# Moving three weight requests in the load order of a chunk-selecting attention and soft-MoE kernel

## The chip, the cores and the metric

The kernel runs on one core of one Trainium2 chip. The metric is device time in microseconds (us), lower is better; a run's figure is the median over its executions. The profiled execution is one more execution of the same program, with its own time and its own span (first to last instruction of the program).

## The reference

Inputs are `q`, `k`, `v` of shape 4 x 8 x 768 x 64 (batch, heads, positions, head size) and the MoE's `phi` (512 x 32), `w1` (8 x 512 x 1024) and `w2` (8 x 1024 x 512), all float32.

```python
# attention: every query keeps the 6 best of 24 chunks of 32 keys
k_min, k_max = min and max of k over each chunk
ub = sum_d max(q * k_min, q * k_max);  ub = where(causal chunk, ub, -1e9)
top_chunks = argsort(ub)[..., -6:]
scores = where(chosen chunk and causal, q @ k.T / 8, -1e9)
attn = softmax(scores) @ v
x = attn as 3072 rows of 512
# soft MoE with 32 slots, 4 to an expert
logits = x @ phi
d = softmax of logits over the rows;   slot_input = d.T @ x
slot_out[e] = relu(slot_input[e] @ w1[e]) @ w2[e]     for the 8 experts
c = softmax of logits over the slots;  out = c @ slot_out
```

## The kernel before

Two heads of one batch form a **pair**; there are 16 pairs, numbered 0 to 15 in the code and here. Written k10 or v3, a load is that of pair 10's `k` or pair 3's `v`; w0 to w15 are the 16 expert weights in the order in which they are asked for (w0 to w7 are `w1`, w8 to w15 are `w2`).

All loads are DMAs that GpSimd (POOL) issues, in the order in which they stand in its instruction stream, and they cast float32 to bf16 on the way. `load(i, "k")` and `load(i, "q")` (L141) fetch 192 KB as written, `load_v(i)` (L149) as much in smaller pieces, `load_w(i)` (L131) 1024 KB. `k_in` and `q_in` have three buffers each, `v_t` four; each of the first 14 weights has its own place, w14 and w15 take the place of pools that are closed near the end. Each issue on POOL also waits until the issue eight before it has landed, since the DMAs take turns on eight semaphores.

The order of work is written out by hand (a manual schedule), engine by engine. A prologue prepares pairs 0 and 1 and makes the masks; then a loop runs i from 1 to 15. Iteration i computes the scores of pair i in six groups (`scores`, L303 and L313; `expo`, the exponential on ScalarE, L327; `mask`, POOL, L337), applies the weights of pair i-1 to `v` (`pv`, L355), chooses the chunks of pair i+1 (`ubound` L255 and L262, `select` L274 to L277, `ns_transposes` L285), transposes and evacuates k and q of pair i+2 (`transposes` L211, `evac_T` L220, `kmin` L229, `kmax` L235), normalises pair i-2 (L368) and asks for k and q of pair i+4 and v of pair i+2. The MoE's steps for a batch run in the iterations after its last pair.

`weights(i)` (L537) asks for as many weights as `wplan` says for iteration i, after `load_v(i + 2)`; the entry 0 is served in iteration 1:

```python
wplan = {0: 1, 2: 1, 3: 1, 4: 1, 5: 1, 7: 1, 8: 1, 9: 1, 10: 1, 11: 1, 12: 1, 13: 2, 14: 1, 15: 1}
```

With w0, asked for in the prologue, that makes 16. After the loop the experts run: `experts_in` (L800) with w0 to w7, `experts_out` (L838) with w8 to w14, `last_expert_out` (L849) with w15. Then the 3072 output rows are formed and written by DMAs from the SyncE queue.

Of the kernel before, what the change touches and what calls it, by code (L numbers as in the profile page):

```python
# [60 lines left out]
def kernel(  # L61
# [69 lines left out]
    def load_w(i):  # L131

        if i < E:
            src = moe_w1[i].rearrange("(a p x) f -> p a (x f)", p=P, x=2)
            dst = w_sb[i].rearrange("p (a f) -> p a f", a=NDG // 2)
        else:
            src = moe_w2[i - E].rearrange("(a p x) d -> p a (x d)", p=P, x=4)
            dst = w_sb[i].rearrange("p (a f) -> p a f", a=NFG // 4)
        nc.gpsimd.dma_start(out=dst, in_=src)  # L139

    def load(i, nm):  # L141

        b, j = divmod(i, NPB)
        t = inp.tile([P, 2, NQT * D], BF16, name=nm + "_in", tag=nm + "_in")
        src = {"k": k, "q": q}[nm][b, 2 * j:2 * j + 2]
        nc.gpsimd.dma_start(out=t, in_=src.rearrange("h (p g) d -> p h (g d)", p=P))  # L146
        st[nm, i] = t

    def load_v(i):  # L149
        b, j = divmod(i, NPB)  # L150
        nc.gpsimd.dma_start(  # L151
            out=v_t[i % NV][:, :, :, :D],
            in_=v[b, 2 * j:2 * j + 2].rearrange("h (g p) d -> p h g d", p=P),
        )
# [14 lines left out]
    for j in range(4):  # L169
# [8 lines left out]
        pattern=[[-CH, 2], [-64, 2], [0, NCHUNK]], channel_multiplier=1,  # L178
    )
    load(1, "q")  # L180
    nc.gpsimd.affine_select(
        out=qgrp, in_=qgrp, compare_op=ALU.not_equal, fill=1.0, base=0,
        pattern=[[-1, 4], [0, CH]], channel_multiplier=1,
# [8 lines left out]
    def spread_mask(t0, t1):  # L192
        nc.scalar.copy(
            smask[:, :, t0:t1].rearrange("p o t a x -> p o (t a) x"),
            schunk[:, :, 4 * t0:4 * t1].broadcast_to([P, 2, 4 * (t1 - t0), CH]),
        )
# [3 lines left out]
    def warm(n):  # L200
        r = ones_sq.rearrange("p (o c) -> p o c", o=1).broadcast_to([P, 4, P])
        for _ in range(n):
            nc.tensor.matmul(warm_ps, lhsT=ones_sq, rhs=r, start=True, stop=True)

    def transposes(i, nm):

        ps = p_tp.tile([P, NQT, P], BF16, name="tr_ps", tag="tp")
        src = st.pop((nm, i))
        for g in range(NQT):
            for h in range(2):  # L210
                nc.tensor.matmul(  # L211
                    ps[h * 64:(h + 1) * 64, g, :], lhsT=src[:, h, g * D:(g + 1) * D], rhs=ident,
                    is_transpose=True,
                )
        st[nm + "ps", i] = ps
# [53 lines left out]
    def select(i):  # L269
        ub = st.pop(("ubps", i)).rearrange("p j h x c -> p (j h x) c")  # L270
        mx = tpu.tile([P, NQT * 2, 8], F32, name="mx", tag="mx")
        for a in range(NQT * 2):
            t = a // 4 + NJ * (a % 2)
            nc.vector.max(mx[:, a, :], ub[:, a, :max(8, 4 * t + 4)])  # L274
        ns = ns_t[i % 2].rearrange("p j h x c -> p (j h x) c")
        nc.gpsimd.tensor_copy(ns[:, :, NCHUNK:NCHUNK + 1], mx[:, :, 0:1])
        nc.vector.tensor_tensor(  # L277
            ns[:, :, :NCHUNK], ub,
            mx[:, :, TOPK - 1:TOPK].broadcast_to([P, NQT * 2, NCHUNK]), op=ALU.is_lt,
        )  # L280
# [250 lines left out]
            step(i // NPB)  # L531


    wplan = {0: 1, 2: 1, 3: 1, 4: 1, 5: 1, 7: 1, 8: 1, 9: 1, 10: 1, 11: 1, 12: 1, 13: 2, 14: 1, 15: 1}
    nw = 1

    def weights(i):  # L537
# [19 lines left out]
    ubound(0)  # L557
    load(3, "k")
    load(3, "q")
    load_v(0)  # L560
    transposes(1, "q")
    evac_T(1, "q")
    spread_mask(NJ, NQT)
    select(0)
    load_v(1)
    warm(5)
    ns_transposes(0)
# [3 lines left out]
    qsplit(1)  # L571
    nc.gpsimd.dma_start(out=phi_sb, in_=moe_phi.rearrange("(hg p) s -> p hg s", p=P))
    make_identity(nc, identf)
    load_w(0)
    load(4, "k")
    load(4, "q")

# [368 lines left out]
```

## Time and profile before

| what | value |
|---|---|
| median of 3 runs | 162.14 us (161.63 to 162.91) |
| profiled execution, its own time | 162.55 us |
| its span | 160.8 us |
| mean granted TensorE clock | 0.979 |
| busy PE, DVE, ACT, POOL | 138.5, 121.4, 122.8, 102.7 us |
| read from HBM, written | 52.49 MB, 6.29 MB |
| DMA queue of the POOL loads | 38416 packets, 26.25 MB as written to the core's memory |

The profile's engines are PE (TensorE matmul), PEld (its weight loads), DVE (VectorE), ACT (ScalarE), POOL (GpSimd) and SP (SyncE). In the timeline a row has start, duration, engine, line, operation, tiles, shape and count, and in brackets how long the engine stood idle before it and what ended that. The DMA issues have the time from the start of the issue to the landing. The table of stretches has each engine's busy time, the granted clock, the busy share of the 16 DMA engines and the GB/s that they wrote.

### The profile page before, as it was taken

What the parts mean: (1) busy time and instruction counts of PE and PEld (TensorE: products, weight loads), DVE (VectorE), ACT (ScalarE), POOL (GpSimd) and SP (SyncE); (2) the same over time, 40 slices, a digit from 0 to 9 for tenths busy, and PEclk for the clock granted to TensorE, in tenths of its full rate; (3) what the DMA queues carried; (4) which work ended last, traced back from release to release, by engine and by line L of the source; (5) the groups of instructions that cost most, each with busy time, mean ns of one, the idle gap of its engine ahead of it and who ended that gap; (6) DMA issues with size and microseconds to landing.
All of it is one profiled execution on the core that took longest, in us unless ns stands there. A gap on an engine that the chain in (4) does not pass through costs nothing.

```text
span 160.8 us, 5896 instructions
## 1 busy us (share of the span) xinstructions
PE 138.5 (86%) x2420; PEld 91.7 (57%) x2420; DVE 121.4 (75%) x433; ACT 122.8 (76%) x169; POOL 102.7 (64%) x203
## 2 busy tenths in 40 slices
PE   7786799999999998999999899969899999987500
PEld 2343366766767686666768576646676854542100
DVE  4465989999999989998988899968862660187620
ACT  3679899999999898999989889968788521166520
POOL 7999577989888696988968986829864800000000
PEclk9999999999999999999999999999999999999965
DMA  3999999999999999999999999999999999329996
GB/s 40 141 120 158 206 197 206 201 182 211 194 210 196 209 200 206 198 182 211 197 210 195 214 191 212 195 207 197 209 203 214 213 217 213 67 71 415 419 419 248
DMA packets 40603, 32.92 MB, mean 205 GB/s; under 512 B 26368, under 2 KB 34816, under 8 KB 40576
## 3 DMA queue, kind: packets, MB, share of 16 engines
q0 software_dynamic: 38416, 26.25, 110.3%
q1 hardware_dynamic: 2160, 6.29, 9.7%
q8 instruction: 19, 0.31, 0.7%
q14 instruction: 8, 0.07, 0.1%
HBM read 52.49 MB, written 6.29 MB: 366 GB/s over the span
## 4 chain that ended last, share of the span: by engine, by line
PE 39%; DMA 23%; ACT 14%; DVE 11%; issue 5%; POOL 4%; DVEq 0%; ACTq 0%; POOLq 0%
DMA k_in<-in_k_dram 15%; ACT e_sb L327 8%; PE sc_ps L303 6%; PE at_ps L355 6%; DMA out_dram<-o_sb 5%; PE sc_ps L313 5%; PE tr_ps L211 4%; PE xT_ps L377 3%; DMA q_in<-in_q_dram 3%; ACT qT L220 3%; DVE mx L274 3%; PE h_ps L800 2%; PE so_ps L838 2%; DVE x_sb L368 2%; PE ub_ps L262 1%
## 5 line engine op out<-in xcount | busy, mean ns | idle before, releaser
L327 ACT ACTIVATE e_sb<-sc_ps 128x1024 bf16<-128x1024 f32 (+1 forms) x96 | 83.1, 917 | 7.1 <-PE sc_ps L313 6.5
L337 POOL TENSOR_SCALAR_AFFINE_SELECT e_sb<-e_sb 128x256 bf16<-128x256 bf16 x96 | 38.1, 414 | 18.5 <-ACT e_sb L327 18.0
L303 PE MATMUL sc_ps<-qT,kT 64*128 64x384 bf16 (+3 forms) x258 | 36.8, 305 | 2.5 <-ACT e_sb L327 1.6
L313 PE MATMUL sc_ps<-nsT,smask 64*128 64x384 bf16 (+2 forms) x294 | 38.1, 284 | 0.1
L355 PE MATMUL at_ps<-v_t,e_sb 128*128 128x65 bf16 x672 | 29.7, 194 | 1.9 <-DVE x_sb L368 1.5
L355 PEld LDWEIGHTS <-e_sb 128*128 128x128 bf16 x672 | 25.6, 98 | 4.1 <-issue 2.6
L274 DVE MAX8 mx<-ub_ps 128x8 f32<-128x8 f32 (+1 forms) x192 | 16.8, 162 | 4.2 <-PE ub_ps L262 4.2
L303 PEld LDWEIGHTS <-kT 64*128 64x128 bf16 x258 | 13.9, 93 | 10.7 <-issue 5.3
L313 PEld LDWEIGHTS <-smask 64*128 64x128 bf16 x294 | 14.9, 94 | 3.9 <-issue 0.6
L151 POOL DMA_DIRECT2D v_t<-in_v_dram x16 | 16.6, 1039 | 0.7 <-PE ns_ps L285 0.5
L229 DVE TENSOR_REDUCE mm<-kT 128x24 bf16<-128x768 bf16 x16 | 15.1, 945 | 2.3 <-ACT kT L220 2.3
L220 ACT COPY kT<-tr_ps 128x768 bf16<-128x768 bf16 x16 | 12.8, 802 | 4.8 <-PE tr_ps L211 4.8
L368 DVE TENSOR_TENSOR x_sb<-at_ps,inv 128x768 bf16<-128x768 f32 (+1 forms) x17 | 15.5, 910 | 0.6
L235 DVE TENSOR_REDUCE mm<-kT 128x24 bf16<-128x768 bf16 x16 | 15.1, 942 | 0.0
L220 ACT COPY qT<-tr_ps 128x768 bf16<-128x768 bf16 x16 | 12.8, 799 | 1.7 <-PE tr_ps L211 1.6
L146 POOL DMA_DIRECT2D k_in<-in_k_dram x16 | 11.7, 733 | 0.9 <-POOLq L930 0.8
L139 POOL DMA_DIRECT2D w_sb<-in_moe_w_dram x16 | 11.4, 711 | 0.9 <-DMA w_sb<-in_moe_w_dram 0.7
L146 POOL DMA_DIRECT2D q_in<-in_q_dram x16 | 11.5, 718 | 0.0
L211 PE MATMUL tr_ps<-ident,k_in 128*64 128x128 bf16 x192 | 8.4, 223 | 2.2 <-DMA k_in<-in_k_dram 1.7
L388 DVE COPY xT_sb<-xT_ps 128x768 bf16<-128x768 bf16 (+1 forms) x15 | 8.0, 536 | 2.6 <-PE xT_ps L377 2.6
L211 PE MATMUL tr_ps<-ident,q_in 128*64 128x128 bf16 x192 | 8.4, 223 | 0.8 <-DMA q_in<-in_q_dram 0.6
L377 PE MATMUL xT_ps<-ident,x_sb 128*128 128x128 bf16 x96 | 8.2, 221 | 0.0
(138 smaller groups left out, 202.7 us busy)
## 6 DMA issues: line engine op xcount, KB each, us to landing
w_sb<-in_moe_w_dram POOLq DMA_DIRECT2D x16, 1024.0 KB, 14.8
out_dram<-o_sb SPq DMA_DIRECT2D x10, 512.0 KB, 4.5
k_in<-in_k_dram POOLq DMA_DIRECT2D x16, 192.0 KB, 10.0
q_in<-in_q_dram POOLq DMA_DIRECT2D x16, 192.0 KB, 10.5
v_t<-in_v_dram POOLq DMA_DIRECT2D x16, 192.0 KB, 10.9
out_dram<-o_sb SPq DMA_DIRECT2D x2, 256.0 KB, 4.3
out_dram<-first SPq DMA_DIRECT2D x2, 128.0 KB, 2.0
out_dram<-first SPq DMA_DIRECT2D x1, 256.0 KB, 2.1
```

Source lines behind the costliest of these rows:

```text
L146: nc.gpsimd.dma_start(out=t, in_=src.rearrange("h (p g) d -> p h (g d)", p=P))
L151: nc.gpsimd.dma_start(out=v_t[i % NV][:, :, :, :D], in_=v[b, 2 * j:2 * j + 2].rearrange("h (g p) d -> p h g d", p=P),)
L211: nc.tensor.matmul(ps[h * 64:(h + 1) * 64, g, :], lhsT=src[:, h, g * D:(g + 1) * D], rhs=ident, is_transpose=True,)
L220: nc.scalar.copy(t.rearrange("d (p g) -> d p g", g=NQT), st.pop((nm + "ps", i)).rearrange("d g p -> d p g"),)
L229: nc.vector.tensor_reduce(mm[:, 0, 0, :], kT, axis=AX.X, op=ALU.min)
L274: nc.vector.max(mx[:, a, :], ub[:, a, :max(8, 4 * t + 4)])
L303: nc.tensor.matmul(ps[:, h, c:c + w], lhsT=kT[r, kg * P:(kg + 1) * P], rhs=qT[r, qs], start=True, stop=False,)
L313: nc.tensor.matmul(ps[:, h, c + (f - t0) * P:c + (l - t0) * P], lhsT=smask[r, x, kg].rearrange("p a b -> p (a b)"), rhs=nsT[r, (f - x * NJ ...
L327: nc.scalar.activation(e[:, :, :w], st.pop(("scps", i, g))[:, :, :w], func=ACT.Exp, scale=scale)
L337: nc.gpsimd.affine_select(out=e[:, :, c:c + P], in_=e[:, :, c:c + P], compare_op=ALU.is_ge, fill=0.0, base=0, pattern=[[0, 2], [1, P]], ch ...
L355: nc.tensor.matmul(o, lhsT=st["e", i, g][:, h, c:c + P], rhs=v_t[i % NV][:, h, kg, :], start=(kg == 0), stop=(kg == t),)
L368: nc.vector.tensor_tensor(st["x", b][:, t0:t1, 2 * j:2 * j + 2, :].rearrange("p t h d -> p h t d"), at[:, :, :, :D], inv.broadcast_to([P, ...
```

## The change

w0 is asked for right behind q1 in the prologue, and no longer behind the identity matrix `identf`. `load_v(0)` goes behind `select(0)`, so that POOL's copy in `select(0)` (L276) comes ahead of v0's request. In `wplan` the weight of iteration 5 goes to iteration 6 and that of iteration 10 to iteration 11, which now has two: w5 is asked for behind k10, q10 and v8 (it was ahead of them), w9 behind k15, q15 and v13. The instructions of all engines are the same in number and kind; only POOL's order differs.

```diff
     load(1, "q")
+    load_w(0)
     nc.gpsimd.affine_select(
         out=qgrp, in_=qgrp, ...
@@
-    wplan = {0: 1, 2: 1, 3: 1, 4: 1, 5: 1, 7: 1, 8: 1, 9: 1, 10: 1, 11: 1, 12: 1, 13: 2, 14: 1, 15: 1}
+    wplan = {0: 1, 2: 1, 3: 1, 4: 1, 6: 1, 7: 1, 8: 1, 9: 1, 11: 2, 12: 1, 13: 2, 14: 1, 15: 1}
@@
     load(3, "k")
     load(3, "q")
-    load_v(0)
     transposes(1, "q")
     evac_T(1, "q")
     spread_mask(NJ, NQT)
     select(0)
+    load_v(0)
     load_v(1)
@@
     make_identity(nc, identf)
-    load_w(0)
     load(4, "k")
     load(4, "q")
```

## The prediction

> **What bounds the kernel now.** I read the page's slices first, then the table of stretches, the waits, the timeline around the waits that DMA ends, and the landings.
>
> ```profile
> DMA  3999999999999999999999999999999999329996
> GB/s 40 141 120 158 206 197 206 201 182 211 194 210 196 209 200 206 198 182 211 197 210 195 214 191 212 195 207 197 209 203 214 213 217 213 67 71 415 419 419 248
> ```
>
> ```profile
> core 0: us, PE busy (x) PEld busy (x) DVE busy (x) ACT busy (x) POOL busy (x), PEclk, DMA share, GB/s
> 3.00:6.50 3.50, 2.46 (x21) 0.83 (x20) 0.49 (x3) 1.10 (x2) 3.33 (x9) 1.00 1.15 159
> 6.50:14.00 7.50, 6.15 (x79) 3.29 (x80) 6.25 (x23) 6.10 (x8) 7.26 (x12) 1.00 1.03 126
> 14.00:25.30 11.30, 9.64 (x172) 6.26 (x171) 8.92 (x39) 10.43 (x14) 8.63 (x19) 1.00 1.61 192
> 25.30:60.00 34.70, 34.12 (x669) 24.50 (x667) 33.19 (x118) 33.66 (x46) 29.35 (x57) 1.00 1.35 202
> ```
>
> A slice is 4.0 us. From 16 us to about 136 us the loads flow at some 200 GB/s without a break: in that stretch the stream of loads is one long queue, and its end depends on how soon it fills. Only the start has room: 126 GB/s from 6.5 to 14 us. PE, ACT and DVE are nearly full as well (34.12, 33.66 and 33.19 of 34.70 us), so the kernel has two chains of like length, loads and compute. They meet at two places in the loop and at the end:
>
> ```profile
> PE tr_ps L211 <- DMA k_in<-in_k_dram: 1.7, 2, 1.3
> POOL w_sb L139 <- DMA w_sb<-in_moe_w_dram: 0.7, 1, 0.7
> ```
>
> ```profile
> 57.90 0.74 POOL L146 DMA_DIRECT2D k_in<-in_k_dram  x1
> 69.18 0.53 PE L211 MATMUL tr_ps<-ident,k_in 128*64 128x128 bf16 x12 [0.37 <-DMA k_in<-in_k_dram]
> 69.75 0.80 ACT L220 COPY kT<-tr_ps 128x768 bf16<-128x768 bf16 x1 [0.20 <-PE tr_ps L211]
> 93.29 0.72 POOL L146 DMA_DIRECT2D k_in<-in_k_dram  x1
> 105.99 0.53 PE L211 MATMUL tr_ps<-ident,k_in 128*64 128x128 bf16 x12 [1.30 <-DMA k_in<-in_k_dram]
> 106.56 0.80 ACT L220 COPY kT<-tr_ps 128x768 bf16<-128x768 bf16 x1 [1.13 <-PE tr_ps L211]
> ```
>
> The requests at 57.90 and 93.29 are k10 and k15. PE stands idle 0.37 and 1.30 us for them.
>
> ```profile
> 118.63 0.77 POOL L139 DMA_DIRECT2D w_sb<-in_moe_w_dram  x1
> w_sb<-in_moe_w_dram POOLq DMA_DIRECT2D x1, 1024.0 KB, 21.5
> 138.07 2.34 PE L838 MATMUL so_ps<-w_sb,hT_pad 128*32 128x512 bf16 x34
> 140.21 0.28 PE L849 MATMUL so_last<-w_sb,hT_pad 128*32 128x256 bf16 x1
> 141.42 0.40 PE L849 MATMUL so_ps<-w_sb,hT_pad 128*32 128x256 bf16 x8 [0.37 <-DVE so_part L881]
> ```
>
> w15 is asked for at 118.63 and lands 21.5 us later, at 140.1; its first user L849 starts at 140.21 behind a PE that was busy with L838. So at the end loads and compute arrive within 0.1 us of each other. This is the main reading: shortening compute alone gains nothing, since w15 lands no sooner, and shortening the loads alone gains nothing, since PE arrives no sooner. The change touches both.
>
> **Part 1, w5 and w9 behind k10 and k15.**
>
> ```profile
> 52.23 0.70 POOL L139 DMA_DIRECT2D w_sb<-in_moe_w_dram  x1 [0.70 <-DMA w_sb<-in_moe_w_dram]
> v_t<-in_v_dram POOLq DMA_DIRECT2D x1, 192.0 KB, 13.0
> w_sb<-in_moe_w_dram POOLq DMA_DIRECT2D x1, 1024.0 KB, 15.9
> k_in<-in_k_dram POOLq DMA_DIRECT2D x1, 192.0 KB, 11.2
> 50.50 1.03 POOL L151 DMA_DIRECT2D v_t<-in_v_dram  x1
> 90.00 0.71 POOL L139 DMA_DIRECT2D w_sb<-in_moe_w_dram  x1
> k_in<-in_k_dram POOLq DMA_DIRECT2D x16, 192.0 KB, 10.0
> ```
>
> The three landings of single requests are v7's (50.50 + 13.0 = 63.5), w5's (52.23 + 15.9 = 68.1) and k10's (57.90 + 11.2 = 69.1): they land in the order of their requests, and a weight takes 4.6 us of the queue. Take it from ahead of k10 and k10 lands at about 64.5, some 4 us before PE asks for it. The same holds for k15, which now stands behind w9 (asked for at 90.00). Both waits go: 0.37 + 1.30 = 1.67 us on PE. ACT, next in line, idled 0.20 and 1.13 us, so if ACT and not PE sets the pace behind the waits the gain is 1.33. I take PE's, since its stream is the fuller one in the table (34.12 of 34.70 us): 1.7. The lower bound is ACT's 1.3; the upper one, 2.4, adds POOL's 0.70 below, if the masks that it held up count after all.
>
> What comes later for it: w5 and w9 themselves, by three loads (about 1 + 1 + 1.5 us by the spacing of the queue) which nobody uses before the experts at 132 us. The loads behind them (k11, v14 and so on) stand behind the same bytes as before. POOL's issue of w5 no longer waits 0.70 us for w3; it held up two masks, for which PE shows no wait, so I book nothing. Without part 2, w15 still lands at 140.1, and the gain would end there: within 0.3 us of nothing.
>
> **Part 2, w0 behind q1.**
>
> ```profile
> 4.75 0.74 POOL L146 DMA_DIRECT2D q_in<-in_q_dram  x1
> q_in<-in_q_dram POOLq DMA_DIRECT2D x1, 192.0 KB, 4.3
> 6.29 0.75 POOL L146 DMA_DIRECT2D k_in<-in_k_dram  x1
> k_in<-in_k_dram POOLq DMA_DIRECT2D x1, 192.0 KB, 5.1
> 12.81 0.72 POOL L139 DMA_DIRECT2D w_sb<-in_moe_w_dram  x1
> 14.23 0.72 POOL L146 DMA_DIRECT2D q_in<-in_q_dram  x1
> q_in<-in_q_dram POOLq DMA_DIRECT2D x1, 192.0 KB, 11.1
> ```
>
> q1 lands at 9.05, k2 at 11.4, q4 at 25.3. What stands between q1 and q4 in the queue is the same set in both kernels: w0, three k, three q, v0, v1 and the small phi. With w0 in front, its 1.05 MB are in the queue from about 6.2 us, and the set needs 4.6 + 6 x 1.0 + 2 x 1.5 + 0.2 = 13.8 us at the rates of the loop, so q4 lands at 22.9: the stream comes **2.4 us sooner**. The other way of counting: 7.5 us at 126 instead of 202 GB/s leave 0.57 MB undone, 2.8 us. Lower bound: nothing gained, if the slow stretch is slow whatever is queued. I take 2.4. Later it is kept: a k lands 10.0 us (median of all 16) after its request, so 2.4 us less still leaves the queue filled. Then w15 lands at 137.7, and PE, 1.7 us sooner, wants it at 138.5: both chains are shorter by at least 1.7.
>
> What it costs at the start:
>
> ```profile
> 9.43 0.53 PE L211 MATMUL tr_ps<-ident,q_in 128*64 128x128 bf16 x12 [0.24 <-ACT kT L220]
> 10.35 0.23 POOL L276 CAST ns_t<-mx 128x12 bf16<-128x12 f32 x1 [0.16 <-DVE mx L274]
> 15.95 0.53 PE L211 MATMUL tr_ps<-ident,k_in 128*64 128x128 bf16 x12
> 14.96 1.49 POOL L337 TENSOR_SCALAR_AFFINE_SELECT e_sb<-e_sb 128x256 bf16<-128x256 bf16 x4
> 17.18 0.23 POOL L276 CAST ns_t<-mx 128x12 bf16<-128x12 f32 x1 [0.73 <-DVE mx L274]
> ```
>
> The issue itself takes POOL 0.72 us. It pushes two masks and the four requests k2 to q3, which end at 9.9 instead of 9.2; v0's issue (1.03 us) now follows the copy at 10.35, which still waits for DVE alone. Cost nothing; had v0 stayed, the copy would be 0.7 late. k2 now lands behind w0: 9.05 + 4.6 + 1.0 = 14.6, wanted at 15.95, 1.3 us to spare. POOL also gets two new waits through the turn of eight: k4's issue for w0's landing (13.7, POOL arrives at about 13.8) and q4's for k2's (14.6, arrives 14.6). Queued behind them are the four masks (1.49 us) and the copy at 17.18, which has 0.73 us of idle time before it. So the cover is about 1 us: if w0 lands at 14.7 or later, chunk choice of pair 1 slips, and PE with it. q1 stands ahead of w0 and has 0.35 us. Taken at nothing; the price if cover fails is the third rival's.
>
> **Sum.** 162.55 - 1.7 = 160.85 for the profiled execution (span 159.1). That execution lies 0.41 above the median of the runs, so the median becomes 160.4.
>
> **Rivals.** *First, the start stays slow* (162.0). When k2 and q2 were in transit, four requests stood in the queue (k2 to q3 were issued by 9.17), and yet 6.5 to 14 us ran at 126 GB/s: that speaks for a limit other than the queue's depth. Then w0 moves 0.62 MB by 14 us, the rest at 202 GB/s, and lands at 16.1; k2 follows at 17.1, 1.1 us late; the set as a whole lands no sooner, w15 stays at 140.1 and eats the 1.7. Against it: the share of 1.03 in that stretch says that each DMA engine had one packet in hand, against 1.35 to 1.61 later, which is what thin queues look like, and w0's large pieces are what fills them.
>
> The Trainium skill has a mechanism for this rival (SBUF — State Buffer, "SBUF: two separate sides"): while VectorE runs certain fast modes, GpSimd cannot write the descriptors of its DMAs, and the DMA engines starve. By that rule the start would be slow for any load, and the sum would be the 162.0 of this rival. The trace bears it out little: DVE is busy 6.25 of 7.50 us in the slow stretch but 33.19 of 34.70 us in one that runs at 202 GB/s.
>
> *Second, slower* (164.3). The slow rate lasts until w0 and k2 have landed: w0 at 9.05 + 1.05 MB / 126 GB/s = 17.4, k2 at 19.0. PE stands 3.0 us at 15.95; POOL issues q4 at 19.0, its masks end at 21.2, and the copy of 17.18 comes 4.0 us late, of which some 0.2 are cover. The start slips 3.9, the loop wins back 1.7: +2.2. It decides from a k2 landing of about 16.7 on (slip over 1.7), and is over 1% from 18.5 on. For it: k2 and q2 landed 2 us apart before, where later ones land 1 us apart. Against: the rate had recovered by 14 us by itself.
>
> **How the numbers follow.** The bound of 1%, 1.62 us, is about what a measurement of this kernel can tell from no change. Forecast 0.60, three quarters of it beyond 1.62 us; the first rival 0.22; the second 0.18. Faster 0.45, same 0.15 + 0.22 = 0.37, slower 0.18. The forecast's own range is 159.7 to 161.1 (gains of 2.4 and 1.3 us, with 0.3 more at the upper end for the spread of a median). The whole range starts just below, at 159.6, holds the first rival and goes to 162.8, into the nearer part of the second.
>
> **What would show it.** Right: no idle time of PE before the transposes of k10 and k15; k2's transposes near 16 us as now; the stretch of 6.5 to 14 us near 200 GB/s; w15's landing near 137.7 and L849 near 138.5. Wrong: an idle PE ahead of k2's transposes, the copy L276 of pair 1 later than 17.4, the stretch still near 126 GB/s, or PE idle before L849 until w15 has landed.

## The result and the profile after

| | median | runs |
|---|---|---|
| before | 161.88 us (161.37 to 162.91) | 4 |
| after | 164.12 us (163.98 to 165.37) | 4 |
| ratio | 1.0141, 95% interval 1.0092 to 1.0189 | |
| profiled execution after | 164.01 us, span 162.3 us, mean clock 0.973 | |

The change makes the kernel 1.4% slower. In a second set (E9 below) twelve runs of it had a median of 164.10 us against 162.36 for the kernel before; the ratio of that set, 1.0066 (1.0032 to 1.01), leaves out runs more than 1.5% above the fastest, so it is the lower of the two. Forecast were 160.4 us, with 162.8 as the upper end; what came is close to the second rival (164.3 us).

From L181 to the prologue's later part a line has a number higher by one in the kernel after (L276 is L277, L285 is L286, L211 is L212); the experts' lines keep theirs. The slices of the page after, 4.06 us each:

```profile
GB/s 39 145 194 190 170 158 86 202 187 190 204 198 208 200 206 184 198 202 203 201 203 204 200 204 185 205 213 202 210 195 217 214 214 215 110 62 406 418 420 250
```

The start is fuller than before (194 and 190 where 120 and 158 stood), but there is a hole where before had none: 86 GB/s in the seventh slice, 24.3 to 28.4 us. The table of stretches, with the columns of before:

```profile
6.50:14.00 7.50, 6.36 (x80) 3.27 (x80) 6.20 (x22) 6.12 (x9) 6.62 (x12) 1.00 1.04 175
14.00:25.30 11.30, 7.80 (x117) 4.75 (x114) 6.43 (x34) 7.88 (x10) 6.56 (x14) 0.85 1.57 158
20.00:21.00 1.00, 0.86 (x13) 0.69 (x15) 0.41 (x2) 0.00 (x0) 1.00 (x4) 0.63 2.14 172
21.00:22.00 1.00, 1.00 (x14) 0.48 (x10) 0.97 (x2) 0.62 (x1) 0.77 (x1) 0.50 1.52 189
24.00:25.00 1.00, 1.00 (x28) 0.79 (x26) 0.97 (x12) 0.87 (x2) 0.65 (x2) 1.00 0.53 37
25.00:26.00 1.00, 1.00 (x20) 0.56 (x18) 0.97 (x3) 0.89 (x2) 0.94 (x3) 1.00 0.18 24
```

The stretch of 6.5 to 14 us runs at 175 GB/s instead of 126, and the next one loses it: 158 instead of 192, with PE busy 7.80 us instead of 9.64 and a mean clock of 0.85. The waits of after name the place:

```profile
PE ns_ps L286 <- POOL ns_t L277: 2.0, 1, 2.0
PE tr_ps L212 <- DMA k_in<-in_k_dram: 1.1, 2, 0.9
```

The largest wait of PE is now one for POOL's small copy in `select(1)`. What made the copy late stands in the landings of single requests (w0's, k2's and w15's) and in the timeline:

```profile
w_sb<-in_moe_w_dram POOLq DMA_DIRECT2D x1, 1024.0 KB, 10.7
k_in<-in_k_dram POOLq DMA_DIRECT2D x1, 192.0 KB, 10.2
w_sb<-in_moe_w_dram POOLq DMA_DIRECT2D x1, 1024.0 KB, 21.8
```

```profile
5.48 0.72 POOL L139 DMA_DIRECT2D w_sb<-in_moe_w_dram  x1
6.99 0.74 POOL L146 DMA_DIRECT2D k_in<-in_k_dram  x1
...
16.72 0.72 POOL L146 DMA_DIRECT2D k_in<-in_k_dram  x1 [2.31 <-PE ub_ps L263]
17.18 0.53 PE L212 MATMUL tr_ps<-ident,k_in 128*64 128x128 bf16 x12 [0.89 <-DMA k_in<-in_k_dram]
17.67 0.71 POOL L146 DMA_DIRECT2D q_in<-in_q_dram  x1 [0.24 <-issue]
18.40 1.49 POOL L338 TENSOR_SCALAR_AFFINE_SELECT e_sb<-e_sb 128x256 bf16<-128x256 bf16 x4
19.85 0.23 POOL L277 CAST ns_t<-mx 128x12 bf16<-128x12 f32 x1
20.14 0.41 PE L286 MATMUL ns_ps<-ident,ns_t 128*128 128x128 bf16 x3 [2.00 <-POOL ns_t L277]
23.85 0.53 PE L212 MATMUL tr_ps<-ident,k_in 128*64 128x128 bf16 x12
24.71 0.71 POOL L139 DMA_DIRECT2D w_sb<-in_moe_w_dram  x1
71.54 0.53 PE L212 MATMUL tr_ps<-ident,k_in 128*64 128x128 bf16 x12
107.53 0.53 PE L212 MATMUL tr_ps<-ident,k_in 128*64 128x128 bf16 x12
120.16 0.77 POOL L139 DMA_DIRECT2D w_sb<-in_moe_w_dram  x1
...
142.02 0.56 PE L849 MATMUL so_last<-w_sb,hT_pad 128*32 128x256 bf16 x8
```

w0 lands at 5.48 + 10.7 = 16.2. POOL stands idle 2.31 us ahead of k4's request and starts it at 16.72, 0.5 us after that landing. The row names PE's L263 as what ended the wait; that is an instance of a wait for several things put down to the wrong one, and E5 below names w0. k2 lands at 17.2, 0.9 us after PE asked for it, and q4's request follows 0.5 us behind that. Only then come the masks (18.40) and the copy (19.85 instead of 17.18), and PE begins its L286 at 20.14. Three rows of before to compare with:

```profile
17.75 0.33 PE L285 MATMUL ns_ps<-ident,ns_t 128*128 128x128 bf16 x3 [0.85 <-DVE ns_t L277]
20.85 0.53 PE L211 MATMUL tr_ps<-ident,k_in 128*64 128x128 bf16 x12
21.64 0.72 POOL L139 DMA_DIRECT2D w_sb<-in_moe_w_dram  x1
```

PE is 2.39 us late at its L286, and 3.00 us late at k3's transposes (23.85 against 20.85): it ran through 20 to 24 us at a clock of 0.50 to 0.66, and E9 below shows what that costs. At k10's transposes it is 2.36 late and at k15's 1.54, and the waits that stood there (0.37 and 1.30 us) are gone; L849 starts 1.81 late and the span is 1.5 longer. POOL's next weight request, w1's, is 3.07 us later than before, and by then the queue has run dry: the 37 and 24 GB/s above.

### The profile page after: what moved, and what is told of

The parts are those of the page before. It is cut to its first block, busy times and chain, and to the rows that moved or that the text cites. A ratio compares the mean times of both kernels' runs of the same rounds, so it can differ in the third digit from the quotient of the medians.

```text
span 162.3 us, 5896 instructions
## 1 busy us (share of the span) xinstructions
PE 140.8 (87%) x2420; PEld 92.6 (57%) x2420; DVE 122.5 (75%) x433; ACT 122.7 (76%) x169; POOL 103.0 (63%) x203
## 4 chain that ended last, share of the span: by engine, by line
PE 44%; ACT 18%; DVE 17%; DMA 7%; issue 6%; POOL 4%; DVEq 0%; ACTq 0%; SPq 0%; POOLq 0%
ACT e_sb L328 11%; PE sc_ps L304 8%; PE at_ps L356 6%; PE sc_ps L314 6%; DMA out_dram<-o_sb 5%; PE tr_ps L212 5%; PE xT_ps L378 3%; ACT qT L221 3%; DVE mx L275 3%; PE h_ps L800 2%; PE so_ps L838 2%; DMA k_in<-in_k_dram 2%; DVE x_sb L369 2%; POOL e_sb L338 2%; PE ub_ps L263 2%
## 5 line engine op out<-in xcount | busy, mean ns | idle before, releaser
L304 PE MATMUL sc_ps<-qT,kT 64*128 64x384 bf16 (+3 forms) x258 | 37.3, 309 | 2.5 <-ACT e_sb L328 1.6
L314 PE MATMUL sc_ps<-nsT,smask 64*128 64x384 bf16 (+2 forms) x294 | 38.7, 288 | 0.1
L304 PEld LDWEIGHTS <-kT 64*128 64x128 bf16 x258 | 14.0, 94 | 10.7 <-issue 5.4
L212 PE MATMUL tr_ps<-ident,k_in 128*64 128x128 bf16 x192 | 8.7, 229 | 1.1 <-DMA k_in<-in_k_dram 1.1
L250 DVE TENSOR_SCALAR qpn<-qT 128x768 bf16<-128x768 bf16 x15 | 9.5, 633 | 0.0
L212 PE MATMUL tr_ps<-ident,q_in 128*64 128x128 bf16 x192 | 8.7, 229 | 0.1
```

The source lines that it names most:

```text
L212: nc.tensor.matmul(ps[h * 64:(h + 1) * 64, g, :], lhsT=src[:, h, g * D:(g + 1) * D], rhs=ident, is_transpose=True,)
L304: nc.tensor.matmul(ps[:, h, c:c + w], lhsT=kT[r, kg * P:(kg + 1) * P], rhs=qT[r, qs], start=True, stop=False,)
L314: nc.tensor.matmul(ps[:, h, c + (f - t0) * P:c + (l - t0) * P], lhsT=smask[r, x, kg].rearrange("p a b -> p (a b)"), rhs=nsT[r, (f - x * NJ ...
```

## The experiments

Unless said otherwise the time is the median, and the ratio is to the kernel before, run on the same chip.

**E1, the new `wplan` alone.** Does part 1 do what it says, and what is it worth by itself?

```diff
-    wplan = {..., 5: 1, 7: 1, 8: 1, 9: 1, 10: 1, 11: 1, ...}
+    wplan = {..., 6: 1, 7: 1, 8: 1, 9: 1, 11: 2, ...}
```

> Only the new wplan (w5 behind k10, w9 behind k15); w0 and v0 stay where they were. Theory A (the loss sits at the start, in what w0's place does): not slower than before; PE's idle time of 0.37 and 1.30 us ahead of the transposes of k10 and k15 is gone, and since w15 still lands near 140.1 the gain ends there: 161.3 to 161.9 against 161.9. Rival B (the moved weights of the loop cost the time): slower by 1 us or more, 163 and up. Rival C (w15's landing does not bound the end): the whole 1.7 us are won, 160.2.

Measured: 161.98 us, ratio 0.9967 (0.9941 to 0.9994). The profiled execution:

```profile
104.60 0.53 PE L211 MATMUL tr_ps<-ident,k_in 128*64 128x128 bf16 x12
140.52 0.40 PE L849 MATMUL so_last<-w_sb,hT_pad 128*32 128x256 bf16 x8 [1.07 <-DMA w_sb<-in_moe_w_dram]
140.74 0.40 PE L849 MATMUL so_ps<-w_sb,hT_pad 128*32 128x256 bf16 x8
```

k15's transposes start at 104.60 with no idle time, where before had 105.99 and 1.30. This execution had been 0.28 us later at k2 (16.23 against 15.95), so the two waits gave 1.39 + 0.28 = 1.67 us. At the end PE waits 1.07 us for w15, and most of the gain is lost again; a part stays, since the second half of L849 starts 0.68 us sooner than before (140.74 against 141.42, which had waited for DVE's `so_part`), and the span is 0.4 us shorter. Part 1 alone is 0.33% faster than before (0.37 us by the medians). Of all versions tried it is the only one whose interval lies below 1, but only just, and with so many versions compared one such interval can be chance.

**E2, the start alone** (w0 behind q1, v0 behind `select(0)`, the old `wplan`).

```diff
     load(1, "q")
+    load_w(0)
...
-    load_v(0)
...
     select(0)
+    load_v(0)
...
-    load_w(0)
     load(4, "k")
```

> Only the start of the change (w0 behind q1, v0's request behind select(0)); the old wplan. Theory A: slower by more than the whole change, as the 3 us that pair 1 slips are not won back at k10 and k15, or by as much where those two waits swallow the slip: 164.0 to 165.0. Rival B (the wplan costs): 161.9 or faster.

Measured: 165.24 us, ratio 1.0165 (1.0122 to 1.0208).

```profile
17.82 0.67 PE L212 MATMUL tr_ps<-ident,k_in 128*64 128x128 bf16 x12 [1.62 <-DMA k_in<-in_k_dram]
20.77 0.50 PE L286 MATMUL ns_ps<-ident,ns_t 128*128 128x128 bf16 x3 [1.53 <-POOL ns_t L277]
```

The time is a little above the expected 164.0 to 165.0. The whole loss sits in part 2; k2 comes 1.62 us late and the selection 3.0 us later than before (20.77 against 17.75).

**E3, the change with k4 and q4 asked for behind `select(1)`.** This takes away the two requests that hold up POOL and leaves w0 where the change puts it.

```diff
     make_identity(nc, identf)
-    load(4, "k")
-    load(4, "q")
...
     select(1)
+    load(4, "k")
+    load(4, "q")
```

> The whole change, but k4 and q4 are asked for behind POOL's copy of select(1) instead of ahead of the masks of pair 0, so that the wait for w0's landing (turn of eight) holds up nothing of pair 1. Theory A1 (the turn of eight on POOL is most of the slip): PE's 2.00 us ahead of ns_transposes(1) go, k2's 0.89 us stay; the slip falls from 3.0 to about 1.0 us and the time to 162.0 to 162.6. Rival A2 (k2's late landing is the slip): no change against the whole change, 164.1.

Measured: 162.82 us, ratio 1.0026 (1.0003 to 1.005).

```profile
17.44 0.23 POOL L277 CAST ns_t<-mx 128x12 bf16<-128x12 f32 x1 [1.17 <-DVE mx L275]
18.01 0.33 PE L286 MATMUL ns_ps<-ident,ns_t 128*128 128x128 bf16 x3 [0.51 <-ACT kT L221]
```

The copy waits for DVE again, as before, and PE's 2.00 us of idle time are gone. The median is 1.3 us below that of the change (164.1 both times). The change was not run beside E3; by the ratios its loss of 0.7% (E9) to 1.4% falls to 0.3%. So most of the loss lay in these two requests, though 162.82 is above the 162.0 to 162.6 that were expected. Against E1 0.8 us are left; this profile shows k2 and q2 late by 0.26 and 0.18 us, and at the end PE waits 0.7 us for w15.

**E4, w0 behind q2 instead of q1.** Of what the start needs, only k3, q3 and the two `v` still stand behind w0.

```diff
     load(1, "q")
-    load_w(0)
...
     load(2, "k")
     load(2, "q")
+    load_w(0)
```

> The whole change, but w0 is asked for behind q2 instead of ahead of k2, so that k2 and q2 land as before and the turn of eight puts k2 and q2, not w0 and k2, ahead of k4 and q4. Theory A: no idle PE ahead of k2's transposes and of ns_transposes(1), no slip; the waits at k10 and k15 are gone and the loads end 1 to 2 us sooner: 160.5 to 161.3. If w0 costs wherever it is early (k3 late, v2 held by w0 through the turn of eight): 162 to 163.

Measured: 162.26 us, ratio 0.9993 (0.9974 to 1.0013). The loss is gone, but the gain did not come. w0 lands at 18.35, 5.28 us behind q2, and w15 at 139.83, 0.3 us sooner than before and not 1 to 2. v0, behind it in the queue, is late:

```profile
21.99 0.54 PE L356 MATMUL at_ps<-v_t,e_sb 128*128 128x65 bf16 x12 [0.62 <-DMA v_t<-in_v_dram]
141.18 0.76 PE L892 MATMUL oh_ps<-so_all,cT_all 128*128 128x256 bf16 x4 [0.19 <-DVE so_all L883]
```

And before, the row with which the output rows begin:

```profile
142.02 0.75 PE L892 MATMUL oh_ps<-so_all,cT_all 128*128 128x256 bf16 x4 [0.20 <-DVE so_all L883]
```

So up to the output rows this execution is 0.84 us ahead of before; its span is only 0.1 us shorter (160.7). The output rows took that much longer in it, and why is open.

**E5, the change with eight more warm-up matmuls ahead of `ns_transposes(1)`**, to see what the lower clock costs.

```diff
+    warm(8)
     ns_transposes(1)
```

> The whole change, and eight dependency-free matmuls (warm) ahead of ns_transposes(1), where PE stood idle for 2.00 us and the granted clock then was 0.50 from 21 to 23 us. The eight results are never read. Theory A (the idle engine's lower clock is a part of the slip, the wait itself the larger one): clock 1.00 from 20 to 24 us, the time 0.3 to 0.7 us better than the whole change, 163.4 to 163.9. Rival (the lower clock is most of the loss): 162.5 or less. Rival (the clock costs nothing): 164.1.

Measured: 162.90 us, ratio 1.0033 (1.0001 to 1.0065).

```profile
16.01 0.72 POOL L146 DMA_DIRECT2D k_in<-in_k_dram  x1 [1.25 <-DMA w_sb<-in_moe_w_dram]
19.43 0.34 PE L286 MATMUL ns_ps<-ident,ns_t 128*128 128x128 bf16 x3
21.00:22.00 1.00, 0.71 (x9) 0.27 (x6) 0.83 (x4) 1.00 (x3) 0.06 (x1) 1.00 1.70 193
22.30 0.53 PE L212 MATMUL tr_ps<-ident,k_in 128*64 128x128 bf16 x12
```

Here k4's request has w0's landing as what released it. The clock stayed at 1.00, and from L286 to k3's transposes PE took 2.87 us, against 3.71 in the profile after and 3.10 before. So the lower clock cost some 0.8 us in the one profiled execution. The median came down by 1.2 us, more than was expected (0.3 to 0.7 us); by the ratios of E5 and E9 it is 0.3%, 0.5 us. The change without them spreads by 3.5 us over the runs of E9, and w0 landed 0.7 us sooner here than in the profile after, so the share of the clock in the median is not settled.

**E6, E4 with q3 asked for behind v0.**

```diff
     load(3, "k")
-    load(3, "q")
...
     load_v(0)
+    load(3, "q")
     load_v(1)
```

> As the run with w0 behind q2, but q3 is asked for behind v0, as v0 landed 0.6 us too late for pv(0) there. Theory A: that 0.6 us wait goes, w15 lands near 139.8 as there, compute arrives about 0.5 us sooner: 161.4 to 161.9, equal to the run of the plan alone or a little better. Rival (w15's landing alone sets the end): as the run with w0 behind q2, 162.2.

Measured: 161.84 us, ratio 0.9982 (0.996 to 1.0004).

```profile
22.22 0.55 PE L356 MATMUL at_ps<-v_t,e_sb 128*128 128x65 bf16 x12
```

The wait for v0 is gone, but PE is no sooner at this row than in E4, and w15 lands at 140.7 and not near 139.8. The time is in the expected range; it cannot be told from before, nor from E1.

**E7, w0 and w1 ahead of everything** (one profile of the kernel before with these two moved), to measure a weight in a queue that is full from the first request. What a start this late costs is not the point.

```diff
+    load_w(0)
+    load_w(1)
     load(0, "k")
...
-    wplan = {0: 1, 2: 1, ...}
-    nw = 1
+    wplan = {2: 1, ...}
+    nw = 2
...
-    load_w(0)
     load(4, "k")
```

> w0 and w1 are asked for ahead of k0; pair 0 starts late, so the time itself says nothing (some 9 us longer). What is read is the spacing of landings at the start, where the queue is now full from the first request. If the stretch up to 14 us is slow whatever is queued: w1 lands 5.3 to 7 us behind w0, and k0, q0 more than 1.0 us apart. If only short queues of small pieces are slow: w1 lands 4.6 to 4.8 us behind w0, k0 and q0 0.95 to 1.0 us apart, as in the loop.

Measured: 172.92 us, one execution.

```profile
w_sb<-in_moe_w_dram POOLq DMA_DIRECT2D x1, 1024.0 KB, 7.9
w_sb<-in_moe_w_dram POOLq DMA_DIRECT2D x1, 1024.0 KB, 12.0
6.50:14.00 7.50, 0.00 (x0) 0.00 (x0) 0.00 (x0) 0.00 (x0) 2.65 (x5) 1.00 1.06 210
17.00:21.00 4.00, 4.00 (x45) 2.15 (x47) 2.24 (x4) 3.03 (x4) 1.86 (x3) 1.00 1.31 200
```

Asked for at 1.31 and 2.15, the two land at 9.3 and 14.2, 4.9 us apart, k0 and q0 follow 0.98 us apart, and 6.5 to 14 us run at 210 GB/s. So this stretch of time isn't slow as such. DVE, ACT and PE stand still in it too (0.00 us busy), but they are at work from 17 to 21 us, and there the loads, most of them asked for before 9.2 us, still move at 200 GB/s: in this run busy engines alone did not slow a queue that was already full.

**E8, w0 between k2 and q2.** k2 comes on time now; the eighth request behind w0 is q4's.

```diff
     load(1, "q")
-    load_w(0)
...
     load(2, "k")
+    load_w(0)
     load(2, "q")
```

> The whole change, but w0 is asked for between k2 and q2: k2 lands as before, while q4's request now waits for w0 through the turn of eight. Theory A1 (that wait on POOL is most of the slip): PE idle ahead of ns_transposes(1) for some 2 us more than before although no k is late, 163.4 to 164.4. Rival A2 (the slip is k2's late landing): no slip, as the run with w0 behind q2, 162.3.

Measured: 165.40 us, ratio 1.0194 (1.0128 to 1.0261).

```profile
15.96 0.53 PE L212 MATMUL tr_ps<-ident,k_in 128*64 128x128 bf16 x12
18.34 0.71 POOL L146 DMA_DIRECT2D q_in<-in_q_dram  x1 [3.48 <-DMA w_sb<-in_moe_w_dram]
20.52 0.23 POOL L277 CAST ns_t<-mx 128x12 bf16<-128x12 f32 x1
20.80 0.50 PE L286 MATMUL ns_ps<-ident,ns_t 128*128 128x128 bf16 x3 [3.88 <-POOL ns_t L277]
```

PE takes k2 at 15.96, as before. Nevertheless this is the slowest version but E7, a microsecond above the expected 163.4 to 164.4: POOL stands 3.48 us at q4's request until w0 has landed, and PE 3.88 us behind the copy.

**E9, the change once more**, twelve runs and a second profile.

> The whole change once more, beside the next run on the same chip. Its first profile had w0 land 6.9 us behind q1; other runs of the same order had 5.7 and 5.9. Theory A: the time goes with that landing, since POOL's wait goes with it: 163.5 to 164.5, PE idle 1 to 2 us ahead of ns_transposes(1) in its profile, granted clock lowered behind it only where PE stood idle that long. Rival (the first result was a disturbance): 162.5 or less.

Measured: 164.10 us (162.02 to 165.52), ratio 1.0066 (1.0032 to 1.01).

```profile
19.68 0.34 PE L286 MATMUL ns_ps<-ident,ns_t 128*128 128x128 bf16 x3 [2.00 <-POOL ns_t L277]
20.00:21.00 1.00, 1.00 (x25) 0.77 (x26) 0.94 (x2) 0.48 (x1) 1.00 (x2) 1.00 2.07 176
22.55 0.53 PE L212 MATMUL tr_ps<-ident,k_in 128*64 128x128 bf16 x12
```

The same 2.00 us of idle time for the same copy, but the clock stays at 1.00, PE takes 2.87 us from L286 to k3's transposes instead of 3.71, and the profiled execution is 163.33 us instead of 164.01. The kernel is the same in both, so the 0.8 us are the clock's. In this execution the slip is 1.70 us at k3's transposes and 0.18 at k15's (106.17): the two waits that part 1 removes pay for nearly all of it, and of the 0.8 us by which the span is longer than before's 0.6 arise in the output rows. The twelve runs spread over 3.5 us, where the 23 of before spread over 2.0.

**E10, E8 with k4 and q4 asked for behind `select(1)`.** If q4's wait is the loss of E8, it goes.

```diff
-    load(4, "k")
-    load(4, "q")
...
     select(1)
+    load(4, "k")
+    load(4, "q")
```

> As the run with w0 between k2 and q2, and in addition k4 and q4 are asked for behind POOL's copy of select(1). The loads stand in the same order in both; only what POOL holds back while it waits differs. Theory A1: the 3.9 us of idle PE go, q2 alone may be late by up to 1 us: 161.9 to 162.7, some 3 us better than that run. Rival A2 (late loads are the slip): as that run, 164 to 165.

Measured: 162.97 us, ratio 1.002 (0.9989 to 1.0052).

```profile
18.39 0.33 PE L286 MATMUL ns_ps<-ident,ns_t 128*128 128x128 bf16 x3 [0.84 <-DVE ns_t L278]
19.48 0.53 PE L212 MATMUL tr_ps<-ident,q_in 128*64 128x128 bf16 x12 [0.77 <-DMA q_in<-in_q_dram]
```

2.4 us of E8's loss, by the medians, go with two lines moved, though w0 lands no sooner (18.5; 17.8 in E8); some 3 us were expected, and 162.97 is above the 161.9 to 162.7. With E3 this shows the mechanism twice: for the larger part not the late load itself, but the requests that wait for its landing and hold POOL meanwhile. What is left is in part the late load: PE waits 0.77 us for q2 here.

## Why the prediction was wrong

**The step that failed is "w0 takes 4.6 us of the queue".** That figure came from the full queue of the loop, and E7 has 4.9 in a full queue. Behind q1 w0 took 6.9 us in the profile after, 6.3 in E2, 5.9 in E3, 5.7 in E5 and 5.8 in E9; behind q2 5.3 (E4) and 5.5 (E6); behind k2 7.5 (E8) and 7.9 (E10). So it landed at 16.2, not at 13.7. The lower bound of part 2 allowed for a slow start, but only as a gain of nothing, not as a loss. The Trainium skill (DMA: Bandwidth & Descriptors, "Anatomy of one DMA — SWDGE (gpsimd) path") fits such a transfer by itself with 2.0 us and 436 GB/s, an estimate of 4.4 us for the 1 MiB that a weight has as written; every one of these runs took longer, and E7's first weight, alone at the head of the queue, took 7.9 us from its request to its landing.

**"Cost nothing" then failed with it.** The cover was put at about 1 us, with the condition that from a w0 landing of 14.7 on the choice of pair 1 slips. The condition was right and came to hold. The first rival had the landings nearly as they came, w0 at 16.1 and k2 at 17.1 (16.2 and 17.1), though by a slow rate that did not last; but it left out the wait on POOL, which the prediction itself had tied to such a landing. The second rival, given 0.18, tells what happened in its order: PE at k2, POOL at q4, the masks, the copy. The larger stall was at k4 (2.31 us; 0.24 at q4), and all its sizes were too large: w0 at 17.4 (16.2 came), the copy 4.0 us late (2.7), the slip 3.9 (3.0 at k3's transposes). That its 164.3 us comes so close is in part luck. Two terms were in no part of the sum: POOL resumes half a microsecond after the landing that it waits for (16.2 to 16.72, 17.2 to 17.67), and the clock fell, some 0.8 us in this profile (E9).

**"The stream comes 2.4 us sooner" failed too.** The stretch named as the sign did rise, from 126 to 175 GB/s. But q4, with the same set of loads ahead of it, landed at 24.8 instead of 25.3: half a microsecond. In the other versions with w0 early, E7 aside, it landed between 24.4 and 26.1. Then a POOL that was 3 us late asked for w1 that much later, and 24 to 26 us ran nearly empty; w15 landed at 142.0, not at 137.7. One reading behind this step was wrong as well: a DMA share of 1.03 was taken for a thin queue, but E7 has 1.06 with a full one, at 210 GB/s. "Later it is kept" took the requests' times as given, while they hang on POOL's progress. E4 and E6, without the stall, show no more: w15 at 139.8 and 140.7. A slow start with nothing held up is the first rival, and its "same" is what these two gave, although in E4's profile PE did not wait for w15 at the end.

**Right were part 1 and the reading of the end.** The two waits gave 1.67 us by E1 (1.7 was forecast), and without part 2 PE stands 1.07 us for w15, so the 1.67 shrink to 0.4 to 0.5 us (0.37 by the medians, 0.33% by the ratio), a little more than the "within 0.3 us of nothing". It is more because w15 and PE met less closely than the first row of L849 says: before, its second half still waited for `so_part` until 141.42, when w15 had long landed.

**Open in part** is why w0 takes 5.3 to 7.9 us where a queue that is full from the first request has 4.9. The packets of the profile after show where the time went; the first line is the stretch from 7.9 to 13.6 us, the second that from 13.6 to 16.2:

```profile
DMA packets 383, 1.09 MB, mean 192 GB/s; under 512 B 21, under 2 KB 138, under 8 KB 383
DMA packets 621, 0.50 MB, mean 192 GB/s; under 512 B 38, under 2 KB 609, under 8 KB 620
```

The packets of 2 to 8 KB are w0's, 256 of 4 KB each: 245 of them (383 - 138) start in the first stretch and the last 11 (620 - 609) in the second, among some 600 small packets of the loads behind it. So the queue moved 192 GB/s, near the loop's 202, and by the forecast 13.7 us nearly all of w0 was under way; but a load has landed only with its last packet, and the later loads went past w0's last ones. In E8 the rate was low as well: 165 GB/s from w0's first packet (9.2 us) to its landing. Why the last packets lag, and why the rate differs, no run shows.

## What to carry to other kernels

Before a large load is moved ahead, list what waits for its landing: not only the readers of its data, but every later request that must wait for it on the issuing engine, and all work queued behind those on that engine. Size its landing with the slowest transfer in that stage, not with the rate of the steady state, and move the held-up requests behind the work that others wait for. A gain in loads counts only if the engine that asks for them keeps its pace.

## What was not expected of the hardware

In the profile after the clock fell to 0.50 behind 2.00 us of idle PE and came back by 24 us; in E9 the same 2.00 us left it at 1.00, and in E8 it was already 0.50 in the idle time itself, from 19 us on, some 2 us after PE had stopped. In E10 it fell as well, though between 14 us and that fall no single idle time was above 0.9 us. The Trainium skill (TensorE: Matmul & The Clock Gate, "What's actually happening") has the clock halved after an idle window of about 3.4 us that runs freely: that it strikes in one run and not in another agrees with a free-running window; that it struck behind 2.00 us, and in E10 behind short pauses, shows that less than 3.4 us of unbroken idle time is enough. The low stretch lasted 3.41 us in the profile after and in E10, and twice that, 6.83 us, in E2 and E8.
